# A fused attention and two-MLP kernel: a table that shifts the keys of a planner's instruction order, names engines for some steps, and splits some projection pieces into high and low halves

## The chip, the cores and the metric

One core of one Trainium2 chip runs the whole program in one launch. The metric is the device time of that core in microseconds (us): the median of three runs of the kernel before is 713.43 us. The engines are TensorE (PE, with its weight loads shown as PEld), VectorE (DVE), ScalarE (ACT), GpSimd (POOL) and SyncE (SP), which issues the DMAs.

## The reference

Three layers, one after the other. The first is attention over 2 batches of 8 heads with 1152 keys and head width 64; pairs of query rows are averaged first, so 576 queries are left per head:

```
q_pool = q.reshape(B, H, S // 2, 2, D).mean(axis=3)
attn = softmax(q_pool @ k.T / sqrt(D)) @ v
x = attn as [1152 tokens, 512]
h = x @ w_in;  g = (a0 + a1 h + a2 h^2 + a3 h^3) / (1 + |b0||h| + |b1| h^2 + 1e-6);  x = g @ w_out      (2048 wide)
xn = x / sqrt(mean(x^2) + 1e-6) * rms_g
out = (silu(xn @ w_gate) * (xn @ w_val)) @ w_out2                                                        (1536 wide)
```

Weights arrive as 64-bit floats and are turned into 32-bit ones on the chip.

## The kernel before, in words

**Attention.** A head pair has 9 score tiles of 128 query rows by 1152 keys, 72 tiles in all. For each tile PE multiplies q by k into one of two score buffers in PSUM (`hid`, line 783), DVE takes the negated row maximum (`nm`, L812), ACT does the exponential into `p` (L818), PE transposes `p` back into the same PSUM buffer by blocks of 64 columns (L834), and DVE or ACT copy the three banks of transposed blocks to `pt` (DVE L869, ACT L866). The next tile but one can use the buffer only when those copies are done. Tiles go in pairs; between the scores and the transposes of a pair stand up to five steps of the product with v (`av`, L938). At the end of a head pair come the tail steps: copies of `av` to `xt` (L619), the division by the row sums (L989, L994), then the high half `x_hi` (L619) and the low half `x_lo = xt - x_hi` (L632), which the next layer reads. POOL and DVE prepare weights beside all this (L175 to L236: absolute value, shifts, high and low halves; most of the later ones are written to DRAM by `s_store` and fetched again).

**The first MLP** works with each number split into a high and a low half. `three` (L515) makes three matmuls for each product: high by high, low by high, high by low (all L525). `project_ops` makes the hidden block of unit `u` (128 of the 2048 hidden columns) in a `hid` buffer of three banks, one per third of the tokens (c0, c1, c2); there are two such buffers, so unit u+2 may start only when all that reads unit u's buffer is done. For units 0 and 1 (`FINE`) each bank is made in four pieces, one per 128 input columns, since the last head pair's `x_hi` and `x_lo` come late. `rational` then evaluates the quotient: the hidden values are read by ACT (L1125, L1128) and by DVE (L1141 `m_q`, L1131 and L1134 `m_p`); L1162, L1156 and L1165 on DVE end it without the buffer; L1173 (ACT) and L1176 (POOL) make `g_hi` and `g_lo`. `out1` multiplies by w_out into one of two `accp` banks, which ACT (L1229, first group of units) or DVE (L1231) adds to `acc`.

**The norm and the second MLP.** `norm` squares and sums `acc`, scales it and makes the halves `x_hi` (L1328) and `x_lo` (L1333 on POOL, L1335 on DVE) again. `gated` makes a gate and a value block by `project_ops`, ACT takes the tanh (L1384), DVE multiplies (L1388, L1410) and makes `g_lo` (L1418); `out2` accumulates into `acc` and stores.

**What sets the order.** Nothing is written in the order in which it runs. Each step is an `Op` with one or more engines that it may use (`ways`: engine, cost, function), a key, the steps that it depends on and the buffers that it takes. `order` walks through time by its own costs: for each engine it takes, among the steps that could start first, the one with the smallest key, and for a step with several ways it takes the engine on which it would end first. The program's instructions are recorded in that order, engine by engine, each queue strictly in order. The core of the choice:

```
        def __init__(self, eng, cost, key, fn, deps=(), bufs=(), other=()):
            self.ways = [(eng, cost, fn), *other]
            self.eng, self.cost, self.key, self.fn = eng, cost, key, fn
...
                picks.append(min(((op.key, op.at, t, op) for t, op in c if t <= t0 + slack))[2:])
```

The tiles' own matmuls in attention are chained in one written sequence (`seq`), so their order on PE cannot change; the k and q transposes (L732), the division's transposes (L985, L971), and everything on the other engines can.

## Time and profile before

| what | us |
|---|---|
| median of 3 runs | 713.43 (713.33 to 717.75) |
| the profiled execution, its own time | 714.59 |
| its span, first to last instruction | 712.8 |
| PE busy in the span | 685.5 |

The span is what the trace covers; the profiled execution took 1.8 us more than it. It lies 1.16 us above the median of the runs. Matmul ends are modelled in the profile, so a wait of PE is read best from the difference of two starts.

### The profile page before, as it was taken

To read this page: it belongs to the slowest core of one execution; us is meant where nothing else is said; L and a number is where in the kernel's file an instruction comes from. 1 tells how busy PE (TensorE), PEld (TensorE's weight loads), DVE (VectorE), ACT (ScalarE), POOL (GpSimd) and SP (SyncE) were. 2 spreads that over 40 slices of the span, in tenths; PEclk is the share of its full clock that TensorE was granted. 3 is DMA by queue.
4 is the path that set the end of the run, shared out by engine and by line. 5 is a ranking of instruction groups with operands and counts; after the bars stand their busy time and mean duration, and the time that the engine had idled before them with its cause. 6 is when DMAs were issued, how large, how long until landed. Compare 5 with 4: busy or idle time off the path is not lost.

```text
span 712.8 us, 13081 instructions
## 1 busy us (share of the span) xinstructions
PE 685.5 (96%) x5257; PEld 593.6 (83%) x5257; DVE 541.0 (76%) x712; ACT 397.2 (56%) x630; POOL 261.4 (37%) x252
## 2 busy tenths in 40 slices
PE   7899999999999999899999999999999999999997
PEld 6666666666766677899999999998999899989996
DVE  5699998989898885998996967956668156845844
ACT  4677777878877875987755645345334132402210
POOL 3022334656654465323331323257235023403500
PEclk9999999999999999999999999999999999999999
DMA  7434334755554535214105004000224212320103
GB/s 222 124 115 128 113 103 151 229 190 181 201 171 144 188 120 198 99 60 147 60 30 177 30 5 152 26 26 1 90 88 148 60 59 89 119 90 29 60 1 132
DMA packets 53900, 77.66 MB, mean 109 GB/s; under 512 B 6480, under 2 KB 36176, under 8 KB 53840
## 3 DMA queue, kind: packets, MB, share of 16 engines
q1 hardware_dynamic: 53840, 76.83, 33.2%
q8 instruction: 41, 0.67, 0.4%
q14 instruction: 19, 0.16, 0.1%
HBM read 62.40 MB, written 14.42 MB: 108 GB/s over the span
## 4 chain that ended last, share of the span: by engine, by line
PE 81%; DVE 9%; ACT 4%; issue 2%; POOL 1%; DMA 0%; SPq 0%; DVEq 0%; POOLq 0%; ACTq 0%
PE hid L525 33%; PE accp L525 22%; PE av L938 9%; PE hid L783 9%; PE hid L834 5%; ACT p L818 3%; DVE pt L869 2%; PE prep L732 2%; DVE nm L812 2%; DVE xt L619 1%; POOL m_u L1289 1%; DVE m_q L1141 1%; PE prep L985 1%; DMA qn<-in_q_dram 0%; POOL x_lo L1333 0%
## 5 line engine op out<-in xcount | busy, mean ns | idle before, releaser
L525 PE MATMUL hid<-x_hi,win_hi 128*128 128x384 f32 x480 | 161.5, 336 | 3.3 <-DVE m_p L1134 1.4
L525 PE MATMUL hid<-x_lo,win_hi 128*128 128x384 f32 x480 | 160.7, 335 | 0.5 <-DVE x_lo L1335 0.5
L525 PE MATMUL hid<-x_hi,win_lo 128*128 128x384 f32 x480 | 160.5, 334 | 0.0
L818 ACT ACTIVATE p<-hid,nm 128x1152 f32<-128x1152 f32 x72 | 87.8, 1220 | 27.0 <-DVE nm L812 26.9
L812 DVE TENSOR_REDUCE nm<-hid 128x1 f32<-128x1152 f32 x72 | 94.8, 1352 | 8.9 <-PE hid L783 7.6
L525 PEld LDWEIGHTS hid<-x_hi,win_hi 128*128 128x128 f32 x480 | 90.2, 188 | 6.3 <-issue 3.5
L783 PE MATMUL hid<-kT,qT 64*128 64x256 f32 (+3 forms) x800 | 93.8, 376 | 0.9 <-DVE pt L869 0.4
L1176 POOL TENSOR_TENSOR g_lo<-m_p,g_hi 128x1152 fp32r<-128x1152 f32 (+1 forms) x20 | 44.9, 2254 | 133.3 <-ACT g_hi L1173 95.0
L525 PEld LDWEIGHTS hid<-x_lo,win_hi 128*128 128x128 f32 x480 | 90.1, 188 | 1.8 <-DVE x_lo L1335 0.8
L525 PEld LDWEIGHTS hid<-x_hi,win_lo 128*128 128x128 f32 x480 | 90.1, 188 | 0.0
L834 PEld LDWEIGHTS hid<-ident,p 64*128 64x128 f32 x1296 | 53.2, 140 | 38.4 <-ACT p L818 13.7
L834 PE MATMUL hid<-ident,p 64*128 64x64 f32 x1296 | 68.1, 231 | 13.3 <-ACT p L818 8.1
L783 PEld LDWEIGHTS hid<-kT,qT 64*128 64x128 f32 (+1 forms) x800 | 69.6, 180 | 8.7 <-DVE pt L869 1.3
L938 PE MATMUL av<-pt,vn 128*64 128x288 f32 x576 | 76.7, 411 | 0.0
L866 ACT ACTIVATE pt<-hid 128x512 f32<-128x512 f32 (+2 forms) x145 | 59.7, 449 | 29.5 <-PE hid L834 29.0
L525 PE MATMUL accp<-g_hi,wout_hi 128*128 128x384 f32 x192 | 64.8, 337 | 3.0 <-ACT acc L1229 1.8
L525 PE MATMUL accp<-g_hi,wout_lo 128*128 128x384 f32 x192 | 64.2, 334 | 0.0
L525 PE MATMUL accp<-g_lo,wout_hi 128*128 128x384 f32 x192 | 64.2, 334 | 0.0
L938 PEld LDWEIGHTS av<-pt,vn 128*64 128x64 f32 x576 | 38.6, 136 | 27.2 <-issue 3.4
L175 ACT ACTIVATE wc<-wraw 128x512 f32<-128x512 f32 x68 | 45.4, 671 | 26.5 <-POOL win_lo L208 14.7
L869 DVE COPY pt<-hid 128x512 f32<-128x512 f32 (+1 forms) x79 | 47.6, 608 | 16.5 <-PE hid L834 15.2
L203 POOL TENSOR_SCALAR win_hi<-wc 128x512 fp32r<-128x512 f32 x22 | 15.2, 691 | 98.8 <-PE hid L525 89.8
(121 smaller groups left out, 1233.1 us busy)
## 6 DMA issues: line engine op xcount, KB each, us to landing
wraw<-in_moe_w_out_dram SPq DMA_DIRECT2D x28, 512.0 KB, 3.5
far<-spill SPq DMA_DIRECT2D x23, 512.0 KB, 3.6
wraw<-in_moe_w_in_dram SPq DMA_DIRECT2D x16, 512.0 KB, 3.8
wraw<-in_moe_w_gate_dram SPq DMA_DIRECT2D x12, 512.0 KB, 3.6
wraw<-in_moe_w_val_dram SPq DMA_DIRECT2D x12, 512.0 KB, 4.1
kn<-in_k_dram SPq DMA_DIRECT2D x16, 288.0 KB, 3.9
vn<-in_v_dram SPq DMA_DIRECT2D x16, 288.0 KB, 3.5
qn<-in_q_dram SPq DMA_DIRECT2D x16, 256.0 KB, 3.3
```

Of the source, the lines that this page charges most:

```text
L175: nc.scalar.activation(c.bitcast(F32), wt["raw", n][:, :, 1].bitcast(F32), AF.Abs, scale=2.0**-112)
L203: eng.tensor_scalar(hi, w_float(n), 1.0, 1.0, op0=ALU.mult, op1=ALU.mult)
L525: ins = nc.tensor.matmul(dst, lhsT=a[x], rhs=b[y], start=first and i == 0 and p == 0, stop=last and i == n - 1 and p == 2,)
L732: seen(nc.tensor.transpose(ps[:, at:at + 128], src, ident))
L783: ins = nc.tensor.matmul(ps[to, j, c:c + x1 - x0], lhsT=qT[2 * pr + h][rows, c0:c0 + to.stop - to.start], rhs=kT[2 * pr + h][rows, x0:x1], ...
L812: nc.vector.tensor_reduce(out=e["nm"], in_=scores(), op=ALU.max, axis=AX.X, negate=True)
L818: nc.scalar.activation(e["p"], scores(), AF.Exp, bias=e["nm"], scale=1.0, accum_out=sums[pr][:, t:t + 1])
L834: ins = nc.tensor.transpose(ps[:, g, c:c + 64], e["p"][rows, 128 * j:128 * j + 128], ident[rows, rows])
L866: return nc.scalar.activation(to, src, AF.Copy)
L869: return nc.vector.tensor_copy(to, src)
L938: nc.tensor.matmul(e["av", h][64 * c:64 * c + 64, 0:QW], lhsT=v_tile[2 * pr + h][:, KEYS[kt], :], rhs=pt[pr, h][:, kt, c * QW:(c + 1) * QW ...
L1176: eng.tensor_sub(g_(1), p_(), g_(0).bitcast(F32))
```

## The change

A string `SHIFTS` has one symbol for each step in the order in which the steps are made, and each symbol is a number of 250-unit shifts that is added to the step's key (P is no shift; the symbols used go from -40 to +40, so up to 10000 units either way, where a tile is 3100 units). A string `WAYS` leaves most steps (a dot) their choice of engine and names the way for 226 of them. In `project_ops`, a piece of units 0 and 1 of the first MLP, and of unit 0 of the second, is now one of two kinds: `HI` with the two matmuls that read `x_hi`, then `LO` with the one that reads `x_lo`; all four `HI` pieces of a bank come before its four `LO` pieces, and a `HI` piece waits for `x_hi` alone (`xhop`).

```diff
+    SHIFTS = (
+        "]ZAOQF(:O/TPHZGUPNQOPjLPR=?P@PKSPcPPXSPKEPPI]8PYLPZPPC]WB<POPTPDRPPYLUCFHLm=JPJLV`*JP1PPXMPP<PPWFKPP"
...
+    WAYS = (
+        "......1.1......1...0......0..........0.1.............1.0.....0.00.....0....0.......1.0..0...0...0..0"
...
         def __init__(self, eng, cost, key, fn, deps=(), bufs=(), other=()):
-            self.ways = [(eng, cost, fn), *other]
-            self.eng, self.cost, self.key, self.fn = eng, cost, key, fn
+            ways = [(eng, cost, fn), *other]
+            way = WAYS[count[0]]
+            self.ways = ways if way == "." else [ways[int(way)]]
+            self.eng, self.cost, self.fn = self.ways[0]
+            self.key = key + 250 * (SYMBOLS.index(SHIFTS[count[0]]) - 44)
...
-            parts = [(c, [kk]) for c in range(NC) for kk in range(KC)]
+            parts = [(c, [kk], by) for c in range(NC) for by in (HI, LO) for kk in range(KC)]
         else:
-            parts = [(c, range(KC)) for c in range(NC)]
+            parts = [(c, range(KC), ALL) for c in range(NC)]
...
+    ALL = ((0, 0), (0, 1), (1, 0))
+    HI, LO = ((0, 0), (1, 0)), ((0, 1),)
...
-            for p, (x, y) in enumerate(((0, 0), (0, 1), (1, 0))):
+            for p, (x, y) in enumerate(by):
...
+            xhop[c, kk] = [o_h]
```

The number of matmuls stays (the same 4,551 are recorded in the program). What the table does to the order is seen at three places. Lines of the changed kernel are 65 to 70 higher than those of the same steps before (L869 is L937 there, L812 is L880, L619 is L687, L989 is L1057, L525 is L590).

On DVE, at the end of the third head pair (tiles 30 to 33; `nm` x2 are the row maxima of a pair of tiles, `pt` the copies of transposed blocks, `wc` weight work), before:

```order
L812 TENSOR_REDUCE nm<-hid 128x1 x2
L180 TENSOR_SCALAR wc<-wc 128x512
L619 TENSOR_SCALAR xt<-av 64x288 x2
L869 COPY pt<-hid 128x8x64
L989 TENSOR_TENSOR xt<-xt,prep 128x512
L994 TENSOR_TENSOR xt<-xt,rxh 64x64 x2
L223 SCALAR_TENSOR_TENSOR wc<-wraw,wc 128x512
L619 TENSOR_SCALAR x_hi<-xt 128x576
L632 TENSOR_TENSOR x_lo<-xt,x_hi 128x576
L812 TENSOR_REDUCE nm<-hid 128x1 x2
```

And now:

```order
L880 TENSOR_REDUCE nm<-hid 128x1 x2
L180 TENSOR_SCALAR wc<-wc 128x512
L223 SCALAR_TENSOR_TENSOR wc<-wraw,wc 128x512
L687 TENSOR_SCALAR xt<-av 64x288
L937 COPY pt<-hid 128x8x64
L687 TENSOR_SCALAR xt<-av 64x288
L937 COPY pt<-hid 128x8x64
L1057 TENSOR_TENSOR xt<-xt,prep 128x512
L880 TENSOR_REDUCE nm<-hid 128x1 x2
```

Four steps of the tail (the two L994, `x_hi` and `x_lo`) have left DVE for POOL, the second copy of `av` stands behind the first copy of `pt`, and `x_lo` no longer stands ahead of the next pair's maxima.

On DVE, where the first MLP begins (the last head pair's tail, then the first steps of `rational` for units 0 and 1), before:

```order
L989 TENSOR_TENSOR xt<-xt,prep 128x512
L619 TENSOR_SCALAR x_hi<-xt 128x576
L632 TENSOR_TENSOR x_lo<-xt,x_hi 128x576
L1141 SCALAR_TENSOR_TENSOR m_q<-m_u,absb,hid 128x384
L1131 TENSOR_TENSOR m_p<-m_p,hid 128x384
```

And now:

```order
L1057 TENSOR_TENSOR xt<-xt,prep 128x512
L687 TENSOR_SCALAR x_hi<-xt 128x576
L1211 SCALAR_TENSOR_TENSOR m_q<-m_u,absb,hid 128x384
L1201 TENSOR_TENSOR m_p<-m_p,hid 128x384 x2
L1204 SCALAR_TENSOR_TENSOR m_p<-m_p,ncoef,hid 128x384
```

The low half of the last pair has gone to POOL, and the reads of the hidden buffers by DVE begin right behind `x_hi`.

On PE, a little later, the first output blocks of `out1` (`accp_4107`, `accp_4113`, `accp_4209` are the first three, the third taking the bank of the first), before:

```order
L525 MATMUL accp_4107<-g_hi_4179,wout_hi_1105 128x384
L525 MATMUL accp_4107<-g_lo_4180,wout_hi_1105 128x384
L525 MATMUL accp_4107<-g_hi_4179,wout_lo_1106 128x384
L525 MATMUL accp_4113<-g_hi_4179,wout_hi_1105 128x384
L525 MATMUL accp_4113<-g_lo_4180,wout_hi_1105 128x384
L525 MATMUL accp_4113<-g_hi_4179,wout_lo_1106 128x384
L525 MATMUL accp_4209<-g_hi_4089,wout_hi_980 128x384
```

And now (`accp_4104` is the first, `hid_4194` the hidden block of unit 4):

```order
L590 MATMUL accp_4104<-g_hi_4142,wout_hi_1130 128x384
L590 MATMUL accp_4104<-g_lo_4143,wout_hi_1130 128x384
L590 MATMUL accp_4104<-g_hi_4142,wout_lo_1131 128x384
L590 MATMUL hid_4194<-x_hi_141,win_hi_4026 128x384
L590 MATMUL hid_4194<-x_lo_145,win_hi_4026 128x384
L590 MATMUL hid_4194<-x_hi_141,win_lo_4027 128x384
```

Twelve matmuls of unit 4's bank c0 now stand between the end of the first output block and the rest of the second; only then comes the third, which needs the first one's bank.

## Rows read from the trace of the kernel before

**Rows 1.** The page, part 1: PE's busy time, share of the span, instructions.

```profile
PE 685.5 (96%) x5257; PEld 593.6 (83%) x5257; DVE 541.0 (76%) x712; ACT 397.2 (56%) x630; POOL 261.4 (37%) x252
```

**Rows 2.** Busy time by stretch: PE, PEld, DVE, ACT, POOL, granted clock, DMA.

```profile
0.00:8.00 8.00, 6.36 (x34) 5.89 (x36) 1.95 (x10) 2.59 (x4) 1.15 (x9) 1.00 0.71 198
8.00:28.00 20.00, 15.13 (x193) 11.43 (x193) 13.32 (x17) 11.54 (x22) 4.55 (x3) 0.91 0.59 173
28.00:265.00 237.00, 227.43 (x2631) 160.39 (x2627) 213.16 (x312) 180.17 (x350) 112.25 (x118) 1.00 0.49 158
265.00:305.00 40.00, 35.58 (x209) 32.09 (x210) 32.21 (x54) 30.79 (x57) 18.51 (x20) 1.00 0.38 132
305.00:470.00 165.00, 163.29 (x936) 161.71 (x936) 138.91 (x130) 99.39 (x93) 44.64 (x21) 1.00 0.24 77
470.00:492.00 22.00, 20.69 (x122) 18.76 (x121) 13.08 (x28) 13.06 (x28) 16.03 (x25) 1.00 0.00 1
492.00:712.80 220.80, 217.02 (x1147) 203.31 (x1145) 128.37 (x166) 59.64 (x80) 64.30 (x58) 1.00 0.24 78
```

**Rows 3.** Timeline of the first 32 us: SP's issues, then DVE (start, duration).

```profile
1.17 0.42 SPq L652 DMA_DIRECT2D kn<-in_k_dram  x1
2.10 0.55 SPq L657 DMA_DIRECT2D qn<-in_q_dram  x1
...
5.50 0.82 DVE L674 TENSOR_TENSOR qp<-qn 128x640 f32<-128x640 f32 x1 [3.85 <-DMA qn<-in_q_dram]
```

**Rows 4.** PE's waits from 28 to 265 us: total, times, longest.

```profile
PE hid L834 <- DVE pt L869: 3.6, 12, 0.5
```

**Rows 5.** Timeline of DVE at the third head pair's end.

```profile
120.22 0.93 DVE L619 TENSOR_SCALAR xt<-av 64x288 f32<-64x288 f32 x2 [0.62 <-PE av L971]
121.18 0.69 DVE L869 COPY pt<-hid 128x512 f32<-128x512 f32 x1
121.78 0.68 DVE L989 TENSOR_TENSOR xt<-xt,prep 128x512 f32<-128x512 f32 x1
122.38 0.45 DVE L994 TENSOR_TENSOR xt<-xt,rxh 64x64 f32<-64x64 f32 x2
...
123.47 0.45 DVE L619 TENSOR_SCALAR x_hi<-xt 128x576 fp32r<-128x576 f32 x1
123.96 1.73 DVE L632 TENSOR_TENSOR x_lo<-xt,x_hi 128x576 fp32r<-128x576 f32 x1
125.61 2.61 DVE L812 TENSOR_REDUCE nm<-hid 128x1 f32<-128x1152 f32 x2
```

**Rows 6.** Timeline of PE at the same place.

```profile
121.92 0.27 PE L834 MATMUL hid<-ident,p 64*128 64x64 f32 x1 [0.46 <-DVE pt L869]
```

**Rows 7.** Timeline of PE where the first MLP begins (idle time in brackets).

```profile
284.83 0.41 PE L525 MATMUL hid<-x_hi,win_hi 128*128 128x384 f32 x1 [1.41 <-DVE m_p L1134]
...
293.33 0.41 PE L525 MATMUL hid<-x_hi,win_hi 128*128 128x384 f32 x1 [0.95 <-issue]
...
302.65 0.44 PE L525 MATMUL accp<-g_hi,wout_hi 128*128 128x384 f32 x1 [1.76 <-ACT acc L1229]
```

**Rows 8.** Timeline of DVE in the same stretch.

```profile
278.62 0.76 DVE L632 TENSOR_TENSOR x_lo<-xt,x_hi 128x576 fp32r<-128x576 f32 x1
...
292.10 1.13 DVE L1134 SCALAR_TENSOR_TENSOR m_p<-m_p,ncoef,hid 128x384 f32<-128x384 f32 x2
```

**Rows 9.** The chain that ended last: start, us, a run of 48 matmuls.

```profile
324.06 8.32 PE hid L525 x48
```

**Rows 10.** Groups by line and shape: busy us, mean ns | idle before.

```profile
L812 DVE TENSOR_REDUCE nm<-hid 128x1 f32<-128x1152 f32 x72 | 94.8, 1352 | 8.9 <-PE hid L783 7.6 <-ACT pt L866 0.6
...
L1388 DVE SCALAR_TENSOR_TENSOR m_p<-m_p,hid 128x1152 f32<-128x1152 f32 x11 | 14.9, 1352 | 20.1 <-ACT m_p L1384 20.1
...
L1384 ACT ACTIVATE m_p<-hid 128x1152 f32<-128x1152 f32 x11 | 12.5, 1136 | 34.3 <-PE hid L525 34.3
...
L632 POOL TENSOR_TENSOR x_lo<-xt,x_hi 128x576 fp32r<-128x576 f32 x6 | 8.8, 1470 | 16.7 <-DVE x_hi L619 16.5
```

More of the change, by code (lines that the diff above doesn't have):

```diff
@@ L289, in attention_moe_moe2_kernel @@
+    SYMBOLS = "".join(chr(i) for i in range(35, 127) if chr(i) not in "\"\\'")
     ops = []
@@ L496, in fetch_ops @@
         wop["turn", kind] = wop[wseq[n]]
-    xop = {}
+    xop, xhop = {}, {}
     xread = {}
@@ L516, in project_ops, with three @@
         return ps, done
-    def three(jobs, first=True, last=True, seen=None):
+    ALL = ((0, 0), (0, 1), (1, 0))
+    HI, LO = ((0, 0), (1, 0)), ((0, 1),)
+    def three(jobs, first=True, last=True, seen=None, by=ALL):
         n = len(jobs[0][1])
         for i in range(n):
-            for p, (x, y) in enumerate(((0, 0), (0, 1), (1, 0))):
+            for p, (x, y) in enumerate(by):
                 for dst, pairs in jobs:
@@ L526, in three @@
                         dst, lhsT=a[x], rhs=b[y],
-                        start=first and i == 0 and p == 0, stop=last and i == n - 1 and p == 2,
+                        start=first and i == 0 and p == 0, stop=last and i == n - 1 and p == len(by) - 1,
                     )
@@ L562, in hidden_tile, with project @@
         return get
-    def project(w, u, c, kks):
+    def project(w, u, c, kks, by):
         hidden_tile(w, u)()
@@ L568, in project @@
         pairs = [([t[:, kk, :] for t in wx], [t[:, kk, CS[c]] for t in (x_hi, x_lo)]) for kk in kks]
-        three([(env[w, u][:, c, 0:CW], pairs)], kks[0] == 0, kks[-1] == KC - 1, lambda ins: bank_access(w, u, c, ins))
+        three(
+            [(env[w, u][:, c, 0:CW], pairs)], kks[0] == 0 and by is not LO, kks[-1] == KC - 1 and by is not HI,
+            lambda ins: bank_access(w, u, c, ins), by,
+        )
     inner = ExitStack()
@@ L757, in head_ops @@
         v_op[i] = lv
-    pt, pt_buf, pt_op, sums, sum_buf, sum_op, xt_ops, xt_buf, x_op = ({} for _ in range(9))
+    pt, pt_buf, pt_op, sums, sum_buf, sum_op, xt_ops, xt_buf, x_op, xh_op = ({} for _ in range(10))
     def tile_ops(i):
@@ L1009, in pair_ops @@
         o_xh = op_any(copy_ways(lambda: xs(0), x_, SQ, fast=True), key + 2000, o_div, [xb])
+        xh_op[b, hp] = o_xh
         x_op[b, hp] = op_any(sub_ways(lambda: xs(1), x_, lambda: xs(0), SQ), key + 2500, [o_xh], [xb])
@@ L1059, in attention_moe_moe2_kernel @@
         for kk in range(KC):
-            xop[c, kk] = [x_op[b, kk] for b in range(B) if b * SQ < (c + 1) * CW and (b + 1) * SQ > c * CW]
+            of = [b for b in range(B) if b * SQ < (c + 1) * CW and (b + 1) * SQ > c * CW]
+            xop[c, kk], xhop[c, kk] = [x_op[b, kk] for b in of], [xh_op[b, kk] for b in of]
     for u in FINE:
```

62 lines of the change are left out of this document (58 added, 4 removed).

## The prediction

> **What bounds the kernel now.** I read the busy times first: PE works for 685.5 of a span of 712.8 us [rows 1], so PE bounds the kernel. The change keeps every matmul, so all that it can win or lose is PE's idle time, 712.8 - 685.5 = 27.3 us. Next the table of stretches [rows 2], because a mean over the whole span does not say where the 27.3 us lie. In each row the length less the first number is PE's idle time: 1.64 us (0 to 8), 4.87 (8 to 28), 9.57 (28 to 265, the attention tiles, where DVE is busy for 213.16 of 237), 4.42 (265 to 305, where attention hands over to the first MLP), 1.71 (305 to 470), 1.31 (the norm) and 3.78 (492 to the end). Of the last I find all after the last matmul, in the final add and store: inside the second MLP PE never waits. Third, the waits and the timelines inside the stretches, for what ends those waits: copies by DVE of the transposed blocks [rows 4], tail work at a pair's end [rows 5, 6], and three separate events where the first MLP begins [rows 7, 8].
>
> The reader should see that this is a kernel 96% full. Even the removal of every wait from 28 to 492 us gives 9.57 + 4.42 + 1.71 + 1.31 = 17.0 us, 2.4%.
>
> **The change part by part.** I add the terms to the profiled execution, 714.59 us, which lies 1.16 us above the median of the runs.
>
> *Start (0 to 28).* SP now issues q's DMA ahead of k's. Before, k's issue stands at 1.17 us and q's at 2.10, and the first work on q waits for that DMA until 5.50 [rows 3]. The most it can gain is the difference of the two issues, 0.93 us; the least is 0, since the first tile needs k too. I take -0.6, nearer to the first, since DVE's wait there names q's DMA.
>
> *Attention (28 to 265).* The order of the tiles' matmuls is a chain and stays; what moves is who does the work between them. Counted over the order of instructions, DVE loses 9 of the 30 copies of `av` to `xt`, two `x_hi`, the six L994 and a few copies of q, and takes ten more of the short `pt` copies, six half ones and two k copies. At the third pair's end the effect is plain [rows 5]: from 120.22 two `xt` copies (0.93 us) hold up the `pt` copy until 121.18, and PE's transpose waits 0.46 us for it [rows 6]; then the division, L994, `x_hi` and `x_lo` (0.68 + 0.45 + 0.45 + 1.73 us = 3.3) put off the next maxima to 125.61. In the new order the first `pt` copy stands between the two `xt` copies, 0.93 / 2 = 0.47 us earlier, which covers the 0.46; of the 3.3 us only the division's 0.68 is left ahead of the maxima. What DVE loses, POOL takes: an `x_lo` costs 1.47 us there [rows 10], and POOL is busy for 112 of 237 us [rows 2], with nothing behind it that PE waits for. ACT's work stays nearly the same (more `xt`, fewer `pt`). DVE loses about 4.4 us in sum. Price: at the least 0, since DVE still has 213.16 - 4.4 = 209 us of work in 237 and a tile needs a maximum of 1.35 us [rows 10] and its copies one after the other; at the most 9.57, all of the stretch's idle time. I take half, -4.8: it is 0.7 us at each of the seven pair ends, near the 0.46 us that one such wait shows, plus what the modelled ends hide. The L834 waits that name DVE's `pt` are 3.6 us in 12 [rows 4], and with them the part of the idle time that the trace ascribes to nothing.
>
> If the copies and tail steps that went to POOL only make POOL and DVE slow each other, this term is 0. The row that speaks for it is DVE's `x_lo`: 1.73 us at 123.96 [rows 5], beside a `wc` step of POOL, and 0.76 us at 278.62 [rows 8], with POOL idle. The row against it is the maximum `nm`, half of DVE's path, which reads PSUM and keeps to 1352 ns over 72 [rows 10] while POOL is busy half of the time. The Trainium skill, page "Perfetto Trace Analysis", section "Optimizing Scalar/DVE Operations", says that GpSimd and VectorE share an SBUF read port, so that moving operations between the two might not help; by that rule this term would be 0 and the sum some 4.8 us higher.
>
> *Where the first MLP begins (265 to 305).* PE waits 1.41 us at 284.83 for DVE's last read of unit 0's buffer, 0.95 at 293.33 for that of unit 1 and 1.76 at 302.65 for an `accp` bank [rows 7]. The last pair's `x_lo` (0.76 on DVE [rows 8]) goes to POOL, where it costs 1.47 [rows 10]; the reads by DVE begin that much earlier, and the first pieces that need only `x_hi` no longer wait for `x_lo` at all, only the four `LO` pieces of a bank do. The head's last `av` steps also come 6 matmuls (6 x 8.32/48 = 1.04 us [rows 9]) earlier. Together 1.8 us for the 1.41. Before, unit 1's buffer was free when DVE ended its last read at 292.10 + 1.13 = 293.23 [rows 8]; in the new order 17 DVE steps stand before its last read, some 0.5 to 0.57 us each (1.13 / 2), so DVE's own work of 9 to 10 us there remains and only the earlier start helps: I count half of that wait as gone. Behind the first output block stand twelve matmuls of unit 4 (2.08 us), more than the 1.76 us that the third block waits for its bank: this one goes. Bounds: 0 (each wait is replaced by another of the same chain) and -4.42. I take half, -2.2, since three waits of 4.1 us shrink but DVE stays the chain's engine: it is busy for 32.2 of 40 us.
>
> *First MLP (305 to 470).* Its idle time is 1.71 us. ACT and DVE steps are regrouped, some `g_lo` move from POOL to DVE. DVE is at 138.91 of 165 us [rows 2], so a queue that gets longer can cost: one more step of 1.35 us in front of an `acc` add at one place gives up to +2. Bounds +2 and -1.71; I take -1.0, nearer the gain, as each `hid` buffer's slack that I counted in matmuls is as long as before or longer.
>
> *Norm (470 to 492).* Four L1289 adds go from POOL to DVE, which is busy for 13.08 of 22 us. Bounds 0 and -1.31; I take half, -0.7.
>
> *Second MLP (492 to the end).* Nothing can be won: PE is full until the tail. It can lose. PE's order puts the next block into a `hid` buffer sooner: between the last matmul of a block and the first of the next but one stood 36 matmuls (36 x 8.32/48 = 6.24 us) at most places; now at three it is 24 (4.16 us), at one 12 (2.08), and at two 24 instead of 44. A gate block's buffer is read by the tanh (1.14 us) and then by DVE (1.35) [rows 10], 2.5 us with the two handovers on top; a value block's by one DVE step, 1.35. So 4.16 us suffice where DVE is free and 2.08 suffice for a value block alone. Bounds: 0 and +8 (six places, each waiting for one more DVE step, 6 x 1.35). I take +0.4, as DVE is busy only 128 of 221 us.
>
> Sum: -0.6 - 4.8 - 2.2 - 1.0 - 0.7 + 0.4 = -8.9 us; 714.59 - 8.9 = 705.7 for an execution like the profiled one, and 1.16 less, 704.5 us, for the median.
>
> **The rivals.**
>
> *Nearly all the waits go.* The table is fine enough (2019 of 2624 steps have a shift) to place each step. For it: each wait that I looked at in 28 to 305 us is met by a move. Against it: DVE at 90% of attention. It gives 713.43 - 17.0 = 696.4 us.
>
> *The attention gain does not come.* DVE stays the pace, or POOL's work slows it; a wait that goes at one tile returns at the next, since two `hid` buffers allow only so much lead. For it: 12 of PE's waits name `pt` [rows 4], and `pt` work on DVE grows by 16 copies. Against it: the pair ends, where 3 us of tail leave the queue. Gain 8.9 - 4.8 = 4.1 us: 709.3.
>
> *Slower: the `hid` buffers of the second MLP.* The six places with less lead lie on a stretch without any wait now. DVE there has weight steps (L180, L208) in strict order with the gate and value steps; if one stands ahead of L1388 or L1410 and itself waits for ACT or for a DMA, the buffer comes free late. For it: DVE's L1388 waits for ACT's tanh 20.1 us in all [rows 10], the mean 1.8 of 11. Against it: 2.08 us of lead stand at one place alone. It decides when the six places cost more than the 9.3 us won elsewhere, 1.6 us each; at 3 us each (tanh and L1388 fully exposed, 2.5, and half a microsecond of handover) it costs 18, and the time is 713.4 - 9.3 + 18 = 722.
>
> **How the numbers follow.** The forecast (a gain of 5 to 12 us) has 0.50 and 704.5 us; nearly all the waits gone 0.17 and 696.4; no gain in attention 0.25 and 709.3; slower by the second MLP 0.08, spread from 713 to 722. A difference of 1%, 7.1 us, is about what a measurement of this kernel can tell from no change, so faster begins below 706.3. The forecast's own spread (701.4 to 708.4) lies for about 0.35 of its 0.50 below that, and with 0.17 and a little of the third case faster has 0.56; slower than 720.6 has 0.03; the rest, 0.41, is within 1%. The range that leaves out no more than two in ten: below, most of the rival with nearly all the waits gone is kept (to 695.5); above, it reaches past the third case to 712.5.
>
> **What would show it.** Right: in the new trace PE's busy time is again 685 to 686 us; the idle time from 28 to 265 is near 5 us, with the waits of L834's successor for `pt` at half their 3.6; DVE's time between the maxima of a pair's end and the next has one division step instead of 3.3 us; the waits at unit 0's and unit 1's buffers are under 1 us each and the wait for the third `accp` is gone; DVE's first wait for q ends by 5.0. Wrong: idle time in the second MLP before the tail, at blocks 26 to 34; DVE steps beside POOL's new ones at 1.7 us where they took 0.7; or PE's busy time itself changed.

## The result and the profile after

The changed kernel takes 707.75 us (median of 6 executions, 706.74 to 711.31), the kernel before in the same comparison 715.01 (6 executions, 713.33 to 718.16): a ratio of 0.990 with a 95% interval of 0.987 to 0.993, 7.3 us less. The forecast was 8.9 us less, with a range to 712.5.

| what | before | after |
|---|---|---|
| the profiled execution, its own time | 714.59 | 706.74 |
| its span | 712.8 | 705.0 |
| PE busy | 685.5 | 683.8 |

Page, part 1, of the changed kernel (answers to [rows 1]):

```profile
PE 683.8 (97%) x5257; PEld 595.3 (84%) x5257; DVE 544.1 (77%) x724; ACT 397.0 (56%) x624; POOL 246.6 (35%) x246
```

The table of stretches of the changed kernel, columns as in [rows 2], with the borders from the third on moved 6 us earlier, since the same work stands there:

```profile
8.00:28.00 20.00, 15.41 (x171) 11.85 (x168) 13.44 (x18) 10.56 (x19) 3.08 (x2) 0.83 0.51 149
28.00:259.00 231.00, 224.99 (x2648) 161.45 (x2647) 201.42 (x303) 182.50 (x352) 120.84 (x135) 1.00 0.51 164
259.00:299.00 40.00, 37.58 (x225) 34.56 (x225) 31.28 (x53) 31.16 (x55) 18.36 (x19) 1.00 0.39 132
299.00:464.00 165.00, 162.52 (x925) 159.71 (x925) 141.61 (x138) 98.28 (x93) 39.10 (x16) 1.00 0.23 77
464.00:486.00 22.00, 21.24 (x128) 19.87 (x127) 16.59 (x35) 13.87 (x30) 13.93 (x23) 1.00 0.00 1
```

DVE has 201 us of work in attention instead of 213, POOL 121 instead of 112. PE's idle time falls in attention (6.01 us against 9.57), at the handover and in the norm, and rises from 299 to 464 (2.48 us against 1.71). The granted clock of the second row is 0.83 where it was 0.91 before.

Two fixed points split the span: the ninth row maximum on DVE, and the first matmul of the first MLP. Of before, then of after:

```profile
36.42 1.36 DVE L812 TENSOR_REDUCE nm<-hid 128x1 f32<-128x1152 f32 x1
265.22 0.44 PE L525 MATMUL hid<-x_hi,win_hi 128*128 128x384 f32 x1 [0.37 <-ACT pt L866]
```

```profile
37.68 1.36 DVE L880 TENSOR_REDUCE nm<-hid 128x1 f32<-128x1152 f32 x1
258.76 0.41 PE L590 MATMUL hid<-x_hi,win_hi 128*128 128x384 f32 x1 [0.89 <-DVE pt L937]
```

So the start loses 1.26 us, attention goes from 228.80 to 221.08 (7.72 less), and from that matmul to the start of PE's last one it is 443.41 us before and 442.01 after, 1.40 less.

The stretch between the two points, before and after, in the columns of [rows 2]:

```profile
36.42:265.22 228.80, 219.12 (x2536) 154.34 (x2533) 207.78 (x304) 174.77 (x339) 110.91 (x118) 1.00 0.49 158
```

```profile
37.68:258.76 221.08, 215.28 (x2537) 154.23 (x2537) 192.36 (x290) 175.35 (x336) 119.06 (x133) 1.00 0.51 164
```

PE's idle time (the length less the first number) goes from 9.68 to 5.80 us. That is only 3.88 of the 7.72; the other 3.84 come out of PE's busy time, with as many matmuls. The ends of matmuls are modelled, so I read this as waiting that the profile counts as work; no run shows it apart.

**Attention.** PE's waits from 28 to 259 us of the changed kernel (total, times, longest):

```profile
PE hid L902 <- ACT p L886: 3.7, 6, 1.5
PE hid L590 <- DVE pt L937: 0.9, 1, 0.9
...
PE hid L902 <- DVE pt L937: 0.2, 1, 0.2
```

The 3.6 us in 12 waits for DVE's `pt` [rows 4] are 0.2 in one. At the third head pair's end DVE now does this (answers to [rows 5]):

```profile
120.07 0.46 DVE L687 TENSOR_SCALAR xt<-av 64x288 f32<-64x288 f32 x1
120.56 0.69 DVE L937 COPY pt<-hid 128x512 f32<-128x512 f32 x1
121.17 0.68 DVE L1057 TENSOR_TENSOR xt<-xt,prep 128x512 f32<-128x512 f32 x1
121.90 2.62 DVE L880 TENSOR_REDUCE nm<-hid 128x1 f32<-128x1152 f32 x2
```

Only the division stands ahead of the maxima, which start 3.71 us earlier than before (121.90, 125.61), and PE has no wait there (0.46 us, [rows 6]).

From the start of the span to the first matmul of the MLP, DVE is busy for 217.07 us instead of 228.65, 11.6 less. Ten copies of `av` fewer (nine went to ACT) are 4.6 us of it; the L994 and two `x_hi` that went to POOL are 2.2. Another 6.0 are weight steps (L180, L184, L190, L223) that are still on DVE and as many as before, but shorter; the remaining changes add about 1. The largest change among them, before and after (busy us, mean ns):

```profile
L223 DVE SCALAR_TENSOR_TENSOR wc<-wraw,wc 128x512 uint32<-128x512 uint32 x21 | 18.2, 865 | 0.4
```

```profile
L223 DVE SCALAR_TENSOR_TENSOR wc<-wraw,wc 128x512 uint32<-128x512 uint32 x21 | 14.8, 705 | 0.5
```

Before, four of the 21 take 1.56 to 1.66 us instead of 0.69, each beside a TENSOR_TENSOR step of POOL; in the new order it is one, 1.08 us. So the steps that stay also meet POOL's work less often. How much of the 7.72 us each of these is worth was not measured.

**The start.** q's DMA lands earlier, k's later: DVE adds q at 4.21 us instead of 5.50 [rows 3], and the first scores start at 7.57 instead of 7.83. The first transposes of k start at 5.28 us instead of 5.04, and those of q stand behind them, at 6.38 in both. Then PE runs at half its clock. Timeline of PE, and the table's row for 12 to 16 us (the clock is its third number from the end), of the changed kernel:

```profile
11.72 0.77 PE L902 MATMUL hid<-ident,p 64*128 64x64 f32 x17 [1.34 <-ACT p L886]
12.99 0.93 PE L902 MATMUL hid<-ident,p 64*128 64x64 f32 x18 [0.49 <-ACT p L886]
13.70 2.44 PE L851 MATMUL hid<-kT,qT 64*128 64x256 f32 x9
```

```profile
12.00:16.00 4.00, 3.51 (x47) 3.04 (x44) 1.64 (x4) 2.31 (x6) 0.24 (x1) 0.68 0.73 214
```

Nine matmuls of the scores take 2.44 us, where eight take 1.08 at full clock in the run with fillers below; 0.68 is the mean of a stretch that is partly at 2.4 GHz and partly at 1.2.

**The handover.** PE's waits of [rows 7] are now these:

```profile
278.23 0.41 PE L590 MATMUL hid<-x_hi,win_hi 128*128 128x384 f32 x1 [1.20 <-DVE m_p L1204]
...
286.97 0.41 PE L590 MATMUL hid<-x_hi,win_hi 128*128 128x384 f32 x1 [1.22 <-issue]
```

The first is 0.2 us shorter, the second 0.3 longer, and the third (1.76 for an `accp` bank) is gone: 4.12 us have become 2.42.

**First MLP.** New waits of about half a microsecond stand here; two of six:

```profile
340.89 0.44 PE L590 MATMUL accp<-g_lo,wout_hi 128*128 128x384 f32 x1 [0.44 <-POOL g_lo L1246]
...
355.57 0.44 PE L590 MATMUL accp<-g_hi,wout_hi 128*128 128x384 f32 x1 [0.40 <-DVE acc L1301]
```

Where two starts are more than 0.15 us further apart than the usual 0.17, the excess sums to 2.4 us before (four places, from 305 to 470) and 3.5 after (six places, from 299 to 464). In the second MLP there is no such place in either kernel.

### The profile page after: what moved, and what is told of

It reads as the page before. It is cut to its first block, busy times and chain, and to the rows that moved or that the text cites. A ratio compares the mean times of both kernels' runs of the same rounds, so it can differ in the third digit from the quotient of the medians.

```text
span 705.0 us, 13072 instructions
## 1 busy us (share of the span) xinstructions
PE 683.8 (97%) x5257; PEld 595.3 (84%) x5257; DVE 544.1 (77%) x724; ACT 397.0 (56%) x624; POOL 246.6 (35%) x246
## 4 chain that ended last, share of the span: by engine, by line
PE 76%; DVE 14%; ACT 7%; issue 2%; POOL 1%; DVEq 0%; ACTq 0%; POOLq 0%
PE hid L590 24%; PE accp L590 19%; PE hid L851 11%; PE av L1006 10%; PE hid L902 7%; PE prep L800 3%; DVE m_q L1211 2%; ACT p L886 2%; DVE m_p L1201 2%; DVE m_p L1204 2%; DVE m_q L1226 2%; DVE nm L880 1%; DVE m_p L1232 1%; ACT m_u L1195 1%; DVE m_p L1235 1%
## 5 line engine op out<-in xcount | busy, mean ns | idle before, releaser
L590 PE MATMUL hid<-x_hi,win_hi 128*128 128x384 f32 x480 | 161.2, 336 | 4.2 <-issue 2.1
L590 PE MATMUL hid<-x_hi,win_lo 128*128 128x384 f32 x480 | 160.6, 335 | 0.0
L590 PE MATMUL hid<-x_lo,win_hi 128*128 128x384 f32 x480 | 155.4, 335 | 0.0
L880 DVE TENSOR_REDUCE nm<-hid 128x1 f32<-128x1152 f32 x72 | 95.1, 1354 | 15.0 <-PE hid L851 14.6
L590 PEld LDWEIGHTS hid<-x_hi,win_hi 128*128 128x128 f32 x480 | 90.2, 188 | 6.6 <-issue 4.5
L590 PEld LDWEIGHTS hid<-x_lo,win_hi 128*128 128x128 f32 x480 | 89.6, 188 | 1.0
L590 PEld LDWEIGHTS hid<-x_hi,win_lo 128*128 128x128 f32 x480 | 90.1, 188 | 0.0
L902 PEld LDWEIGHTS hid<-ident,p 64*128 64x128 f32 x1296 | 52.7, 140 | 34.8 <-issue 13.7
L1246 POOL TENSOR_TENSOR g_lo<-m_p,g_hi 128x1152 fp32r<-128x1152 f32 (+1 forms) x16 | 37.8, 2368 | 125.8 <-ACT g_hi L1243 79.4
L902 PE MATMUL hid<-ident,p 64*128 64x64 f32 x1296 | 66.2, 230 | 9.0 <-ACT p L886 8.3
L934 ACT ACTIVATE pt<-hid 128x512 f32<-128x512 f32 (+2 forms) x129 | 57.4, 473 | 24.7 <-PE hid L902 23.0
L590 PE MATMUL accp<-g_hi,wout_hi 128*128 128x384 f32 x192 | 65.3, 340 | 1.2 <-DVE acc L1301 1.2
L937 DVE COPY pt<-hid 128x512 f32<-128x512 f32 (+2 forms) x95 | 50.5, 548 | 18.7 <-PE hid L902 17.0
L590 PE MATMUL accp<-g_lo,wout_hi 128*128 128x384 f32 x192 | 64.3, 335 | 0.4 <-POOL g_lo L1246 0.4
L590 PE MATMUL accp<-g_hi,wout_lo 128*128 128x384 f32 x192 | 64.2, 335 | 0.0
L1455 ACT ACTIVATE m_p<-hid 128x1152 f32<-128x1152 f32 (+1 forms) x14 | 14.0, 997 | 57.9 <-PE hid L590 57.8
```

The lines of the kernel that those rows point to most:

```text
L590: ins = nc.tensor.matmul(dst, lhsT=a[x], rhs=b[y], start=first and i == 0 and p == 0, stop=last and i == n - 1 and p == len(by) - 1,)
L880: nc.vector.tensor_reduce(out=e["nm"], in_=scores(), op=ALU.max, axis=AX.X, negate=True)
L902: ins = nc.tensor.transpose(ps[:, g, c:c + 64], e["p"][rows, 128 * j:128 * j + 128], ident[rows, rows])
L934: return nc.scalar.activation(to, src, AF.Copy)
L937: return nc.vector.tensor_copy(to, src)
L1246: eng.tensor_sub(g_(1), p_(), g_(0).bitcast(F32))
```

## The experiments

Twelve kernels ran. A number of the table is an entry's place in it, in the order in which the steps are made: 0 to 1393 belong to the first order (attention, prepared weights, first pieces of units 0 and 1), 1394 to 2623 to the second (both MLPs and the norm).

### The two halves of the table

```diff
-    (the whole table)
+    SHIFTS = SHIFTS[:1394] + "P" * 1230; WAYS = WAYS[:1394] + "." * 1230
```

> The changed kernel with the table cut off behind the first of the two orders (attention, the prepared weights and the first pieces of units 0 and 1 keep shifts and engines; all steps of the first MLP, the norm and the second MLP have none). Theory (the gain is made in attention, by the copies that PE waited for): the first MLP's first matmul starts at 258.8 us as in the changed kernel, 6.4 earlier than before; behind it the waits of the kernel before come back (1.9 us for the accp bank, 2.2 from 305 to 470), so the span is 705.5 to 707 and the time 6 to 7 us under the kernel before. Rival (the two halves of the table need each other): the time is within 3 us of the kernel before.

Measured: 706.32 us, ratio 0.988 (0.986 to 0.989), the whole gain. The first matmul of the first MLP starts at 255.54, 3.3 us before the expected place, since the clock stayed at 1.00 from 8 to 28 us in the profiled execution; for the same reason the span, 704.2, lies under the expected range. The start-to-start excess behind it is 4.2 us at the handover (4.9 before by the same count), 2.4 in the first MLP and 2.0 in the norm, as before. The theory holds: the gain is made in attention. From that matmul to the start of PE's last one it takes 444.50 us here, with a fall of the clock at 294, and 442.01 with the whole table: the second half of the table is worth 2.5 us at most, less than the executions of one kernel differ, and the times do not show it.

```diff
-    (the whole table)
+    SHIFTS = "P" * 1394 + SHIFTS[1394:]; WAYS = "." * 1394 + WAYS[1394:]
```

> The changed kernel with the table cut off in the first order and kept in the second (first MLP, norm, second MLP). Theory: attention is as in the kernel before, the first matmul of the first MLP starts at 265.2 within 0.5 us; of the later 1.6 us (2.1 at the handover, -1.3 in the first MLP, 0.8 in the norm) some 1 to 2 remain: span 711 to 712, the time 1 to 2 us under the kernel before. Rival (halves need each other, or the second half is worth more than the trace of the changed kernel shows): 4 us or more under the kernel before.

Measured: 720.10 us, ratio 1.007 (1.005 to 1.009): slower, a miss for both. The first matmul starts at 266.9, 1.2 us past the expected range: from 8 to 28 us the granted clock is 0.83 in this profiled execution, 0.91 in that of the kernel before [rows 2], with the same order of attention. Behind it the excess grows: 1.84 and 2.43 us at units 0 and 1, and this at 412 us:

```profile
407.97 2.66 POOL L1246 TENSOR_TENSOR g_lo<-m_p,g_hi 128x1152 fp32r<-128x1152 f32 x1 [11.11 <-ACT g_hi L1243]
...
407.97 3.87 DVE L1232 SCALAR_TENSOR_TENSOR m_p<-m_p,ncoef,m_u 128x1152 f32<-128x1152 f32 x1
411.77 0.54 DVE L1301 TENSOR_TENSOR acc<-acc,accp 128x384 f32<-128x384 f32 x1
```

L1232 takes 1.41 us elsewhere. It starts in the same hundredth as POOL's `g_lo`, ends 1.2 us behind it, and the `acc` add for which PE waits 2.46 us stands behind it. The clock then falls to 0.5 around 414 us.

### The split alone

```diff
+    SHIFTS = "P" * len(SHIFTS); WAYS = "." * len(WAYS)
```

> The kernel before with only the HI and LO pieces (no shifts, all engines free). Theory: at the head of the first MLP PE waits for DVE's reads of the hidden buffers, not for x_lo, so the split by itself moves the end by less than 0.7 us: span 712.1 to 713.2. Rival (the split is what shortens the handover from attention to the first MLP, 2.1 us in the changed kernel): span 710.7, 2 us under the kernel before.

Measured: 715.78 us, ratio 1.001 (0.999 to 1.003). The wait at unit 0 is 0.72 us instead of 1.41 [rows 7], those at unit 1 and at the `accp` bank are as before. The theory holds in that the high and low pieces by themselves are worth 0.7 us at one place; the time shows no gain, and the profiled span, 715.8, is outside the expected 712.1 to 713.2, since the clock fell in it for 10 us from 19 and again at 305 us.

### Shifts alone, engines alone

```diff
+    WAYS = "." * len(WAYS)
```

> The changed kernel with its shifts but without the named engines (each step takes the engine on which it would end first). Theory (DVE's time between the maxima at the pair ends is what gave the attention gain, and it takes shifts and names together): DVE keeps 26 of the 28 copies of av and four of the six L994, so about half of the gain is left: the first MLP's first matmul starts at 260 to 263 us (before 265.2, changed 258.8), time 3 to 5 us under the kernel before. Rival (the shifts alone do it): it starts at 259.5 or earlier, and the time is within 2 us of the changed kernel.

Measured: 725.91 us, ratio 1.016 (1.013 to 1.019).

```diff
+    SHIFTS = "P" * len(SHIFTS)
```

> The changed kernel with the named engines but no shifts. Theory as for the shifts alone: about half of the attention gain, first matmul of the first MLP at 260 to 263 us, time 3 to 5 us under the kernel before. Rival (the names alone do it, since they take the tail steps from DVE): 259.5 us or earlier. Second rival (names without the shifts that fit them put steps in each other's way): 265 us or later, time not under the kernel before.

Measured: 729.45 us, ratio 1.020 (1.017 to 1.023). In attention the theory holds for both: the first matmul starts at 261.1 and 262.2 (with shifts alone the clock also fell once, from 17.8 us, by my estimate up to 1.7 us of the 261.1; with engines alone it did not fall there). The time is a miss: each loses some 10 us at the handover. PE, then DVE, of the kernel with shifts alone:

```profile
290.19 0.66 PE L590 MATMUL hid<-x_hi,win_hi 128*128 128x384 f32 x1 [9.44 <-DVE m_p L1204]
```

```profile
282.62 0.79 DVE L180 TENSOR_SCALAR wc<-wc 128x512 uint32<-128x512 uint32 x1 [2.56 <-ACT wc L175]
...
284.35 0.61 DVE L1211 SCALAR_TENSOR_TENSOR m_q<-m_u,absb,hid 128x384 f32<-128x384 f32 x1
```

A weight step (L180) stands on DVE ahead of the first read of the hidden buffers and waits for ACT, which waits for POOL's chain of spilled weights. That is the mechanism of the slower rival, at another place. PE's clock is at 0.5 from 284, while PE still waits, to 294.

### The clock at the start

```diff
+    SHIFTS = SHIFTS[:21] + "P" + SHIFTS[22:]; WAYS = WAYS[:19] + "." + WAYS[20:]
```

> The changed kernel with two entries of the table changed: the two q transposes of head 1 get no shift and the copies of the piece ahead of them choose their engine, so that the transposes stand again between the first two tiles' transposes of p, in the 0.49 us in which PE waits. Theory (the granted clock falls at 13.7 us because PE idles at 11.7 and again at 13.0): the second scores run at full clock again, nine of their matmuls take 1.1 us instead of 2.44, the third maximum starts at 15.1 us instead of 16.41, and the whole gains 1.2 us, span 703.8 of 705.0. Rival (the clock falls at that time whatever PE did just before): the clock from 12 to 16 us stays near 0.68, the third maximum stays within 0.3 us of 16.4, span 705.0 within 0.4.

Measured: 708.92 us, ratio 0.990 (0.989 to 0.992). The transposes stand in the 0.49 us, and the clock falls at the same place:

```profile
12.62 0.44 PE L800 MATMUL prep<-ident,qp 128*128 128x128 f32 x2
13.19 0.87 PE L902 MATMUL hid<-ident,p 64*128 64x64 f32 x18
13.85 2.44 PE L851 MATMUL hid<-kT,qT 64*128 64x256 f32 x9
```

My theory in this form fell: the moved transposes are not the cause. (The profiled span, 708.9, is outside what theory and rival expected, because this execution also has the wait of 2.46 us that the second half of the table had at 412 us, here at 402.) The next kernel asks about all waits of that stretch together:

```diff
     def f_warm():
+        fill.append(T("av", [128, 512], F32, space=PSUM))
...
         def f_T():
+            for _ in range((5, 1, 5, 1, 4)[i] if i < 5 else 0):
+                nc.tensor.matmul(fill[0][:, 0:128], lhsT=ones, rhs=ones, start=True, stop=True)
```

> The changed kernel with 16 more matmuls (ones by ones, into the av bank, read by nobody) in the waits of PE ahead of the first five tiles' transposes. Theory (the granted clock falls between 12 and 28 us because PE has idled there): the clock stays at 1.00 from 8 to 28 us, the third maximum starts at 14.6 to 15 us instead of 16.41 and the ninth at 34.5 to 35.5 instead of 37.7; the median falls by 1.5 to 3 us to 705 to 706. Rival (the clock falls there whatever PE does, or the added matmuls delay the transposes by what they save): the third maximum stays at 16.2 or later and the median within 0.7 us of 707.75 or above.

Measured: 706.65 us (704.24 to 708.80), ratio 0.987 (0.985 to 0.990). From 8 to 28 us the clock is 1.00; one of its rows, and PE in it:

```profile
12.00:16.00 4.00, 3.93 (x58) 3.39 (x52) 2.58 (x5) 2.47 (x6) 0.00 (x0) 1.00 0.74 220
```

```profile
11.73 0.77 PE L902 MATMUL hid<-ident,p 64*128 64x64 f32 x17 [0.28 <-ACT p L886]
12.43 0.49 PE L907 MATMUL av<-ones 128*128 128x128 f32 x2
12.99 0.78 PE L902 MATMUL hid<-ident,p 64*128 64x64 f32 x18
13.61 1.08 PE L851 MATMUL hid<-kT,qT 64*128 64x256 f32 x8
```

The third maximum starts at 15.06, the ninth at 34.94 (37.68 without the fillers), the first matmul of the MLP at 256.01: 2.75 us earlier. The median did not fall as far as expected. The profiled execution (708.80) met the 2.4 us of 412 us above, here at 396:

```profile
394.40 3.87 DVE L1237 SCALAR_TENSOR_TENSOR m_p<-m_p,ncoef,m_u 128x1152 f32<-128x1152 f32 x1
...
394.40 2.65 POOL L1251 TENSOR_TENSOR g_lo<-m_p,g_hi 128x1152 fp32r<-128x1152 f32 x1 [11.11 <-ACT g_hi L1248]
...
398.79 0.56 PE L590 MATMUL accp<-g_hi,wout_hi 128*128 128x384 f32 x1 [2.27 <-DVE acc L1306]
```

Two more of the six lie at 707.74 and above; that they met it too is likely, but they were not profiled.

The same fillers in the kernel before:

> The kernel before (no table, no split) with the same 16 matmuls in PE's waits ahead of the first five tiles' transposes. Theory (the kernel before loses clock at the start in most executions, as the changed one does, and the two orders differ by some 9.5 us without that): the clock stays at 1.00 from 8 to 28 us, the median is 712.8 to 714, against 714.8 to 715.6 of the kernel before, and 9 to 10 us above the 704.2 of the changed kernel with both additions. Rival (the start costs clock in the changed order only): the median stays within 0.5 us of the kernel before in the same call.

Measured: 714.68 us, ratio 0.9986 (0.9973 to 0.9998), against 715.86 beside it, so the rival falls. None of the 12 executions with the matmuls has a mean clock under 0.997; of the 17 without, 11 have. Over all profiles of this study the clock stays at 1.00 from 8 to 28 us in each of the five with the matmuls, and in three of the nine without. That is the best evidence here that PE's waits let the clock fall at the start. The clock is 1.00 from 8 to 28 us and the first matmul of the MLP starts at 263.82 instead of 265.22. The median is 0.7 above the expected range, and 10.5 above the 704.20: in the profiled execution the clock falls at 300 to 305, behind the wait of 1.76 us for the `accp` bank, so that wait is paid twice. To the first matmul of the MLP the two orders, both with the fillers, are 7.81 us apart (263.82 and 256.01).

### Who starts first at 397 us

In the changed kernel's own profile DVE is first, by 0.01 us, and PE waits for nothing; the step that suffers is another (DVE, then POOL):

```profile
397.16 1.41 DVE L1232 SCALAR_TENSOR_TENSOR m_p<-m_p,ncoef,m_u 128x1152 f32<-128x1152 f32 x1
398.49 0.55 DVE L1301 TENSOR_TENSOR acc<-acc,accp 128x384 f32<-128x384 f32 x1
398.96 3.36 DVE L1226 SCALAR_TENSOR_TENSOR m_q<-m_q,m_u 128x1152 f32<-128x1152 f32 x1
...
397.17 3.94 POOL L1246 TENSOR_TENSOR g_lo<-m_p,g_hi 128x1152 fp32r<-128x1152 f32 x1 [11.12 <-ACT g_hi L1243]
```

```diff
             def f_lo(eng=nc.gpsimd):
+                if u == 10:
+                    nc.gpsimd.tensor_copy(scratch, g_(0)[:, 0:64].bitcast(F32))
```

> The changed kernel with one small copy (128x64) on POOL ahead of unit 10's g_lo (L1246), so that this g_lo starts about 0.3 us later. In the profile of the changed kernel it starts at 397.17 us, 0.01 behind DVE's L1232 (1.41 us), and DVE's step after the next takes 3.36; in the runs in which both start in the same hundredth, L1232 takes 3.87 and PE waits 2.45 us for the acc add behind it. Theory (whichever of the two engines starts first keeps the other out, and POOL wins in part of the executions): now DVE is always first, no execution has the 2.45 us, the profile shows L1232 at 1.41 us and PE's wait at 399 us gone, and the median falls by 1 to 2 us against the changed kernel's 707.75, with no execution above 709.5. Rival (the long L1232 comes from something else, or the block only moves): the spread and the median stay within 0.7 us of the changed kernel's.

Measured: 704.80 us (703.73 to 705.13), ratio 0.985 (0.983 to 0.987): 3 us under the changed kernel's median, which was not measured again beside it (the kernel before took 715.48 here, 715.01 there), and all five executions within 1.4 us. DVE, then POOL:

```profile
395.20 1.43 DVE L1233 SCALAR_TENSOR_TENSOR m_p<-m_p,ncoef,m_u 128x1152 f32<-128x1152 f32 x1
...
395.18 0.24 POOL L1248 COPY scratch<-g_hi 128x64 f32<-128x64 f32 x1 [11.10 <-ACT g_hi L1244]
395.37 3.78 POOL L1249 TENSOR_TENSOR g_lo<-m_p,g_hi 128x1152 fp32r<-128x1152 f32 x1
```

The copy takes 0.24 us, `g_lo` starts 0.17 behind DVE, and the theory holds. What it saves where POOL would have been first can be read from two kernels that are alike there: from the matmul behind the `acc` wait at 394 us to the norm's first, at 470, it is 75.91 us in the changed kernel's profile and 79.77 in the first of the clock experiments, which has the wait of 2.46 us and a fall of the clock behind it: 3.9 us. The median fell by more than the expected 1 to 2 us, and part of that is not the port: in the profiled execution the clock did not fall at the start either, but only from 151 us. How the 3 us divide between the two is not shown.

### Both additions, and two more edits

> The changed kernel with both additions: the 16 matmuls in PE's waits before 28 us, and the small POOL copy ahead of unit 10's g_lo. Theory (the spread of the changed kernel is the fall of the clock at the start and the port at 397 us, and each is met by its addition): clock 1.00 from 8 to 28 us, no wait of 2.45 us near 397, span 701 to 702.5, median 703 to 704.3, all executions within 2 us; 11 to 12 us under the kernel before. Rival (the two are the same loss seen twice, or the clock falls later instead): median 704.8 or above, no better than the POOL copy alone.

Measured: 704.20 us (703.64 to 705.83), ratio 0.985 (0.983 to 0.987). The median is in the expected range, but not clearly under the 704.80 of the POOL copy alone, so the rival (no better than the POOL copy alone) is not ruled out. No wait of 2.45 us stands near 397. The profiled span, 703.7, is above the expected 701 to 702.5, and the executions differ by 2.2 us instead of 2: the clock is 1.00 from 8 to 28 us but falls at 150, behind a wait that has no fillers:

```profile
150.38 1.22 PE L902 MATMUL hid<-ident,p 64*128 64x64 f32 x17 [1.52 <-ACT p L886]
```

It is the fastest version of this study. The three executions with a mean clock of 1.000 take 703.64 to 704.06; those of the kernel before with a clock of 0.999 or 1.000, over all comparisons, take 713.1 to 713.6. So with full clock, and with DVE first at 397 us, the orders lie 9.5 us apart; the traces give 7.81 to the first matmul of the MLP and 1.40 behind it, 9.2.

```diff
+    K = [*range(1394), *range(1669, 1795), *range(2223, 2295)]
+    SHIFTS = "".join(c if i in K else "P" for i, c in enumerate(SHIFTS))
+    WAYS = "".join(c if i in K else "." for i, c in enumerate(WAYS))
```

> The changed kernel with the 16 matmuls, and with the table switched off for the steps of units 5 to 15 of the first MLP, for all of out1, for the weight and fetch steps of the second order and for the second MLP; on for attention, units 0 to 4 and the norm. Theory (the table's shifts between 305 and 470 us cost 1.1 us against the order without it, those at the handover and in the norm gain 1.4 and 0.7): waits of PE in the MLPs of 6.4 us in sum instead of 7.5, no wait of 2.45 us at 397 since the order there is another, span 700.5 to 702, median 702.3 to 703.8. Rival (the shifts of the parts fit only each other): waits of 9 us or more, median above 705.

Measured: 709.19 us, ratio 0.992 (0.989 to 0.995): the rival. One wait costs what was to be won:

```profile
334.61 0.41 PE L590 MATMUL hid<-x_hi,win_hi 128*128 128x384 f32 x1 [3.78 <-issue]
...
333.10 1.40 DVE L1209 SCALAR_TENSOR_TENSOR m_p<-m_p,ncoef,hid 128x1152 f32<-128x1152 f32 x1
```

DVE's last read of the hidden buffer ends at 334.5, with six steps of two units in front of it on the queue since 323.95, the first of them 2.78 us long beside POOL's `g_lo`. I read this as shifts of units 0 to 4 that fit only the rest of the table; it was not tried unit by unit.

```diff
+    WAYS = "".join("1" if i - 286 in range(0, 787) and (i - 286) % 112 < 3 else c for i, c in enumerate(WAYS))
```

> The changed kernel with the 16 matmuls, and with the tail of the first seven head pairs (the two L1062, x_hi and x_lo) named for DVE, as many of them stood before. Theory (tail work on DVE between two pairs' maxima is what PE waited for): DVE gets 5 more x_lo, 6 more x_hi and 14 L1062, some 1.7 to 2.6 us at each of the seven pair ends; the first MLP's first matmul starts 2.5 to 6 us later than with the 16 matmuls alone (256.0), at 258.5 to 262, and PE waits for DVE's pt again in several places. Rival (the tail lies in DVE's idle time, and the attention gain comes from the places of the copies alone): it starts at 257.2 or earlier.

Measured: 721.75 us, ratio 1.009 (1.006 to 1.012). The first matmul of the MLP starts at 261.39, 5.4 us later than with the fillers alone, in the expected range (the edit reached the eighth pair too, which comes behind that matmul and bears on the handover alone); the clock fell once on the way, at 88 to 92 us, which I estimate at up to 1.7 us (2 us at 0.50 and 2 at 0.64), so 3.7 or more are the tail's. PE's waits from 28 to 265 us:

```profile
PE hid L902 <- ACT p L886: 4.4, 5, 1.8
PE hid L902 <- DVE pt L939: 1.0, 3, 0.4
...
```

The waits for DVE's `pt` are back in three places. Two things limit what this shows. It puts 28 tail steps of seven pairs on DVE, where the kernel before had 10 and the changed one 3, so it is more than the change undone; DVE's time to the first matmul of the MLP, 227.52 us, is about that of before (228.65). And even so the matmul starts 2.4 us earlier than in the kernel before with the same fillers (263.82), 4.1 without the fall of the clock: with as much work on DVE, the places and engines of the rest, the copies of `av` and `pt` among them, keep about a third to a half of the gain. So the rival holds in part. The other 8 us of this kernel are lost behind attention, where its waits at the handover are up to 3.15 us.

## Why the prediction was right, and where not

**The sum was near, but by errors that cancel, and that is luck.** Terms of the two profiled executions, 7.85 us apart:

| term | forecast | measured | by which reading |
|---|---|---|---|
| start | -0.6 | +1.3 | to the ninth maximum, 36.42 and 37.68 |
| attention | -4.8 | -7.7 | from there to the first matmul of the MLP |
| handover | -2.2 | -1.7 | waits of 4.12 and 2.42 us |
| first MLP | -1.0 | +1.1 | excess of starts, 2.4 and 3.5 us |
| norm | -0.7 | -0.8 | excess of starts, 2.1 and 1.3 us |
| second MLP | +0.4 | 0 | no excess in either |

- Start: the step that failed is "I take -0.6, nearer to the first, since DVE's wait there names q's DMA". DVE's add did come 1.29 us earlier, but k's DMA came later, and the first scores gained 0.26. The trace named the last wait of one engine, and the next one behind it was k, as the lower bound said. What the forecast did not have at all is the clock: it fell in this stretch in the profiled execution, which I estimate (one less the granted clock, times its time) at 3.4 us after and 1.7 before. The fillers show that it is PE's waits that let it fall; in the two executions compared it costs 2.75 us to the first matmul of the MLP. It is not the change that made it fall more often: with the changed kernel's attention and no fillers it stayed up to 28 us in two other profiled executions (the first half of the table alone, and the POOL copy), and with the attention of before it was 0.83 in one (the second half alone). The +1.3 of the table is the luck of two executions. With the fillers in both kernels the ninth maximum starts at 35.03 before and 34.94 after, and attention takes 228.79 and 221.07: the start is worth 0.1 us, and attention 7.7 as above.
- Attention: the wait was named rightly, but two steps of the sizing failed. One is "all that it can win or lose is PE's idle time", with the 9.57 us as the most: PE's idle time fell by 3.88 us, near the half that I took, and another 3.84 came out of PE's busy time, which I had only as "plus what the modelled ends hide", without a number; my own sign of being wrong, a changed busy time (683.8 where I named 685 to 686), came true. The other is "DVE loses about 4.4 us in sum": it lost 11.6, and 6.0 of them are steps that did not move, a term that I did not have. The rival that POOL and DVE slow each other came out the other way round, since they met less often. The waits for `pt` went from 3.6 to 0.2 us. Tail steps put on DVE, more than before, bring 3.7 to 5.4 us back, and 2.4 to 4.1 stay. With full clock shifts and named engines together reach 255.5; engines alone reach 262.2, and shifts alone 261.1, or some 259.4 by the estimate without their fall of the clock: it takes both.
- The rule of the Trainium skill, page "Perfetto Trace Analysis", section "Optimizing Scalar/DVE Operations", would have put attention at 0. The trace differs there: POOL's work there grew from 112.25 to 120.84 us, DVE's maxima kept 1.35 us, and the stretch is 7.7 us shorter. But most of what left DVE went to ACT, so this is no test of that rule alone.
- Handover: of the three waits, the third went as the order said. The first two were to lose 1.41 and half of 0.95 and did not: DVE's reads began 1.9 us earlier against the first matmul (12.2 behind it, 14.1 before), but 12 steps and pauses for ACT now stand before the read that PE waits for, where it had been 10. The split alone shortens the first wait to 0.72, with the whole change it is 1.20. The forecast's sign of under 1 us for both waits failed.
- First MLP: the step that failed is "I take -1.0, nearer the gain, as each `hid` buffer's slack that I counted in matmuls is as long as before or longer". Of the six new waits four name DVE's `acc` adds and POOL's `g_lo`, 2.3 of the 3.5 us, which I had only in the upper bound. The other two, 1.2 us, are at `hid` buffers, each ended by DVE's last read, so the slack counted in matmuls did not cover that either (0.85 us before).
- The slower rival came true in no place of the second MLP. Its mechanism, a weight step that waits for ACT in front of a read, did come at the handover when the named engines were taken away: 9.4 us at one place.

**Why the median gained less than the order is worth.** With full clock the two orders lie 9.5 us apart, the medians 7.3. All six executions of the changed kernel have a mean clock of 0.993 to 0.998. Which of them met POOL's `g_lo` first at 397 us is open, as only one was profiled, and in that one DVE was first. With that order settled by the POOL copy no execution of two kernels takes more than 705.83.

**What stays open.** Whether the 704.2 of both additions differs from the 704.8 of the one; what the copies of `av` that went to ACT, the tail steps that went to POOL and the shorter weight steps are worth each; and why the second half of the table costs 4 us without the first, which was read at three waits, not tested one by one.

## What to carry to other kernels

Compare orders by fixed points of the program (the ninth maximum, the first matmul of a stage) and not by the time alone: the clock's falls moved single executions by more than most of the terms of the sum. Do not take PE's idle time for the most that an order can win: here half of the gain in attention lay in its busy time. A table fitted as a whole is one object: a part that looks worthless by its waits can be what another part rests on. Where an off-path engine is released at the same moment as a step on the path and both read two operands from SBUF, give one of them a clear lead; 0.2 us were enough here.

## What I had not expected of the hardware

- A hundredth of a microsecond decides 2.4 us. POOL's `g_lo` and DVE's L1232 or L1226 (each with two operands in SBUF) run one after the other: POOL first, DVE takes 3.87 instead of 1.41; DVE first, POOL takes 3.94 instead of 2.65 and DVE's next step of that kind 3.36, while the `acc` add between them, which reads `accp` from PSUM, keeps 0.55. Seven profiles have these two steps at the same moment: in four DVE takes 3.87, in three (the changed kernel and the two with the POOL copy) 1.41 to 1.44. The Trainium skill, page "SBUF — State Buffer", section "SBUF: two separate sides", says that whichever of the two starts first holds the shared port pair for the whole instruction; the trace agrees.
- The granted clock fell from 2.4 to 1.2 GHz behind single waits of PE (1.34 and 0.49 us ahead of 13.7 us, 1.52 at 150, 2.27 at 398), but not each time: with the same program in attention it fell at 13.7 us in one profiled execution and not at all before 294 in another. The wait of 2.46 us at 402 so costs 3.9 us, with the fall behind it.
- 16 matmuls that nobody reads, in waits that PE has anyway, kept the clock at 1.00 from 8 to 28 us in all five profiles that have them; without them it stayed in three of nine. By the first MLP that gave 2.75 us against an execution in which the clock had fallen (0.83), and 1.40 in the kernel before (0.91); with the POOL copy in place the two medians, 704.20 and 704.80, do not differ clearly.
